# Attention visits of four and three tiles, one sigmoid split by banks, and PV with crossed heads, in a fused sigmoid-attention and SwiGLU kernel

## Chip, cores, metric

One core of one Trainium2 chip. The metric is device time in microseconds (us), the median of the runs of one kernel. Times of different kernels are compared through runs on the same chip in the same rounds.

## The reference, cut to what matters

```python
# q, k, v: (8 batches, 12 heads, 448, 64); w_gate, w_val: (768, 1536); w_out: (1536, 768)
scores = q @ k.T / sqrt(64) - log(448)
x      = sigmoid(scores) @ v                 # heads side by side: (3584, 768)
g      = x @ w_gate
out    = (g * sigmoid(g) * (x @ w_val)) @ w_out
```

Sigmoid attention has no row sums, so each tile of scores is independent: QK on TensorE, a sigmoid on ScalarE, PV on TensorE.

## The kernel before

Work comes in head groups `n` (four heads of one batch, 24 in all). A group has seven QK tiles of 64 keys each (per tile four 64x64 products side by side in the array), seven sigmoids, one PV. FFN units (`ffn1`: 12 matmuls into two banks, a gate on ScalarE and VectorE; `ffn2`: 24 matmuls) fill TensorE, and between them the program inserts *visits*: a few QK tiles, with PV of the group that was finished last.

All products write into a ring of four PSUM buffers of two banks each. A buffer can be written again once its readers are done.

```python
def attn_step(group, pvs):                     # one visit
    for part in (group[:2], group[2:]):
        scs = [(n, c, qk_tile(n, c)) for n, c in part]
        while pvs:
            pv(pvs.pop(0))
        for n, c, sc in scs:
            sig_tile(n, c, sc)                 # one ACTIVATE over both banks

def pv(n, two=False, at=None):
    ...
    out=P[h2 * 64:(h2 + 1) * 64, w, :S]        # head (h2, w): partitions by h2, bank by w
    ...
    for h2 in range(2):                        # x of a head pair wants partitions by w
        for w in range(2):
            x[w*64:(w+1)*64] <- P[h2*64:(h2+1)*64, w]      # four copies of 64x448
                # two (only the third PV): w == 1 on ScalarE, declared independent of w == 0

visits = [tiles[i:i + 3] for i in range(0, len(tiles), 3)]
...
    fn(*args)                                  # the FFN unit after a visit
    while post:
        trans_pe(post.pop())                   # Q, K of head groups 4 to 6 transposed on TensorE
```

Groups 0 to 2 run in a hand-ordered start, groups 3 to 5 beside the first batch's FFN; from group 7 on the transposes are done by DMA.

Of the kernel before, what the change touches and what calls it, by code (L numbers as in the profile page):

```python
# [10 lines left out]
FP16 = mybir.dt.float16  # L11
BF16 = mybir.dt.bfloat16
SIGM = mybir.ActivationFunctionType.Sigmoid
# [4 lines left out]
def kernel(  # L18
# [10 lines left out]
    nc = tc.nc  # L29
    ctx.enter_context(tc.manual_schedule())  # L30

    B, H, S, D = q.shape
    DM = H * D
    DFF = moe_w_gate.shape[1]
    C = S // D
    NJ = H // 4
    NP = H // 2
# [6 lines left out]
    qkscale = 1.0 / math.sqrt(D)  # L44
# [9 lines left out]
    xtp = ctx.enter_context(tc.tile_pool(name="xtp", bufs=12))  # L54
# [4 lines left out]
    sb_t = one.tile([128, 1], FP32, tag="sbias")  # L59
# [72 lines left out]
    def load(n, which, eng=None):  # L132
        st = stg.tile([128, 2, S], FP32, tag="stg", name=f"st{which}_{n}")
        (eng or nc.sync).dma_start(out=st, in_=src_of(n, which))  # L134
        qkv_st[(n, which)] = st

    def load_v(n):
        t = v16p.tile([128, 2, S], FP16, tag="v16", name=f"v16_{n}")
        nc.gpsimd.dma_start(out=t, in_=src_of(n, 2))  # L139
        v16[n] = t  # L140

    def cast(n, which, eng, lo=0, hi=C):
        st = qkv_st[(n, which)]
        if hi == C:
            qkv_st.pop((n, which))
        t = c16.tile([128, hi - lo, 2, D], BF16, tag="c16" if hi - lo == C else f"c16_{lo}", name=f"c16_{which}_{n}")
        q16[(n, which, lo)] = t
        eng.tensor_copy(  # L148
            out=t.rearrange("p c h d -> p h c d"),
            in_=st.rearrange("p h (c d) -> p h c d", c=C)[:, :, lo:hi, :],  # L150
        )

    def trans_dma(n, which):
        t = q16.pop((n, which, 0))
        d = qkT.tile([128, C, 128], BF16, tag=f"T{which}", name=f"T{which}_{n}")
        nc.sync.dma_start_transpose(out=d, in_=t.rearrange("p c h d -> p (c h d)"))
        for c in range(C):
            qT[(n, which, c)] = d[:, c]
        if which == 0:
            qT[(n, 0)] = d  # L160

    def trans_pe(n, parts=((0, 0, C), (1, 0, C))):

        D2 = Banked()
        ps = D2.t.bitcast(BF16).rearrange("p w (c i) -> p w c i", c=8)
        for i, (which, lo, hi) in enumerate(parts):
            t = q16.pop((n, which, lo))
            for c in range(hi - lo):
                D2.write(
                    nc.tensor.transpose(  # L170
                        out=ps[:, i, c, :], in_=t[:, c].rearrange("p h d -> p (h d)"), identity=idn
                    ),
                    i,
                )
        for i, (which, lo, hi) in enumerate(parts):
            tag = f"T{which}" if hi - lo == C else f"T{which}_{lo}"
            d = qkT.tile([128, hi - lo, 128], BF16, tag=tag, bufs=None if hi - lo == C else 1, name=f"T{which}_{n}_{lo}")
            D2.read(nc.vector.tensor_copy(out=d, in_=ps[:, i, :hi - lo, :]), i)  # L178
            for c in range(lo, hi):
                qT[(n, which, c)] = d[:, c - lo]  # L180
            if which == 0:
                qT[(n, 0)] = d
# [3 lines left out]
    xT = {}  # L186

    def qk_tile(n, c):
        sc = Banked().t
        qt, kt = qT[(n, 0)], qT[(n, 1, c)]  # L190
        for w in range(2):
            for h2 in range(2):
                r = slice(h2 * 64, h2 * 64 + 64)
                nc.tensor.matmul(  # L194
                    out=sc[w * 64:(w + 1) * 64, h2, :S],
                    lhsT=kt[r, w * 64:(w + 1) * 64],
                    rhs=qt[r, :, w * 64:(w + 1) * 64],
                    start=True,
                    stop=True,
                )  # L200
        return sc

    def sig_tile(n, c, sc):
        pt = ptp.tile([128, 2, S], FP16, tag="pt", name="pt")
        nc.scalar.activation(out=pt, in_=sc[:, :, :S], func=SIGM, bias=sb_t, scale=qkscale)  # L205
        pts[(n, c)] = pt

    def pv(n, two=False, at=None):
        b, j = divmod(n, NJ)
        P = Banked(at=at).t  # L210
        vt = v16.pop(n)
        for c in range(C):
            pt = pts.pop((n, c))
            for h2 in range(2):
                for w in range(2):
                    r = slice(w * 64, w * 64 + 64)
                    nc.tensor.matmul(  # L217
                        out=P[h2 * 64:(h2 + 1) * 64, w, :S],
                        lhsT=vt[r, h2, c * D:(c + 1) * D],
                        rhs=pt[r, h2, :],  # L220
                        start=(c == 0),
                        stop=(c == C - 1),
                    )
        for h2 in range(2):
            x = xtp.tile([128, S], FP16, tag="xT", name=f"xT_{b}_{2 * j + h2}")
            for w in range(2):
                o, i = x[w * 64:(w + 1) * 64, :], P[h2 * 64:(h2 + 1) * 64, w, :S]
                if two and w == 1:
                    cp = nc.scalar.copy(out=o, in_=i)
                    tc.declare_no_dep(cp.ins, group=f"half{n}_{h2}", reason="other partitions")  # L230
                else:
                    cp = nc.vector.tensor_copy(out=o, in_=i)  # L232
                    if two:
                        tc.add_to_no_dep_group(f"half{n}_{h2}", cp.ins)
            xT[(b, 2 * j + h2)] = x


    hT = {}
# [1 line left out]
    def ffn1_mm(D, b, f, prs):  # L240
        cs = slice((f % FW) * 128, (f % FW) * 128 + 128)
        for i, w16 in enumerate((wg16, wv16)):
            for pr in prs:
                D.write(
                    nc.tensor.matmul(  # L245
                        out=D.t[:, i, :S], lhsT=w16[f // FW][:, pr, cs], rhs=xT[(b, pr)],
                        start=(pr == 0), stop=(pr == NP - 1),
                    ),
                    i,
                )  # L250
# [92 lines left out]

    FIRST, PER = f1_end[0] - 5.0, 38.5
    tiles = [(n, c) for n in range(NJ, NQ) for c in range(C)]
    visits = [tiles[i:i + 3] for i in range(0, len(tiles), 3)]
    vtime = []
    for grp in visits:
        n, c = grp[0]
        b, j = divmod(n, NJ)  # L350
# [6 lines left out]
    def attn_step(group, pvs):  # L357
        for part in (group[:2], group[2:]):
            scs = [(n, c, qk_tile(n, c)) for n, c in part]
            while pvs:  # L360
                pv(pvs.pop(0))
            for n, c, sc in scs:
                sig_tile(n, c, sc)

    NPE = 2 * NJ + 1

# [1 line left out]
    V, G = nc.vector, nc.gpsimd  # L368
# [4 lines left out]
    for i in range(9):  # L373
        nc.tensor.matmul(out=ring[i % 4][:, i // 4 % 2, :], lhsT=warm[:, :128], rhs=warm, start=True, stop=True)
    cast(0, 0, V)
    cast(0, 1, V, 0, 2)
    trans_pe(0, ((0, 0, C), (1, 0, 2)))
    cast(0, 1, V, 2, C)

    def fetch(n):  # L380
        load(n, 0, G)
        load(n, 1, G)
        load_v(n)

    def ready(n):
        cast(n, 0, G)
        cast(n, 1, G)
        if n >= NPE:
            trans_dma(n, 0)
            trans_dma(n, 1)  # L390

    def chunk(n, c):
        sig_tile(n, c, qk_tile(n, c))
# [48 lines left out]

    k0 = ring_at[0] % 4
    early = [Banked("f")]
    for prs in (range(2), range(2, NP - 2)):
        ffn1_mm(early[0], 0, 0, prs)
    chunk(2, 5)
    chunk(2, 6)
    early.append(Banked("f"))
    ffn1_mm(early[1], 0, 1, range(NP - 2))  # L450
# [9 lines left out]

    post = []
    begin = {(n, c): [] for n in range(NJ, NQ) for c in (0, 4)}
    begin[(3, 0)] += [lambda: post.append(4)]
    begin[(3, 4)] += [lambda: ready(5)]
    begin[(4, 0)] += [lambda: post.append(5), lambda: fetch(6)]
    begin[(4, 4)] += [lambda: ready(6)]
    begin[(5, 0)] += [lambda: fetch(7)]
    begin[(5, 4)] += [lambda: post.append(6)]
    begin[(6, 0)] += [lambda: ready(7), lambda: fetch(8)]
# [15 lines left out]
    for dur, fn, args in units:  # L485
        if vi < len(visits) and tcur >= vtime[vi]:
            group = visits[vi]
            vi += 1
            pvs, pend = pend, []
            attn_step(group, pvs)  # L490
            for n, c in group:
                for act in begin.get((n, c), ()):
                    act()
                if c == C - 1:
                    pend.append(n)
        if pend and (
            fn is ffn1 and args[1] == 0 and (args[0], NP - 1) not in xT
            or vi == len(visits) and tcur >= vtime[-1] + 4.0
        ):
            for n in pend:  # L500
                pv(n)
            pend = []
        fn(*args)
        while post:
            trans_pe(post.pop())
        tcur += dur


# [28 lines left out]
```

## Time and profile before

| | |
|---|---|
| time, median (6 runs) | 434.64 us |
| span of the profiled run | 433.3 us |
| TensorE / VectorE / ScalarE busy | 418.9 / 220.6 / 209.9 us |
| sigmoids of scores | 168, mean 1006 ns |
| PV copies 64x448 on VectorE | 94, mean 622 ns |

The prediction below shows the lines of the profile and how they are read.

### The profile page before, as it was taken

What the parts mean: (1) busy time and instruction counts of PE and PEld (TensorE: products, weight loads), DVE (VectorE), ACT (ScalarE), POOL (GpSimd) and SP (SyncE); (2) the same over time, 40 slices, a digit from 0 to 9 for tenths busy, and PEclk for the clock granted to TensorE, in tenths of its full rate; (3) what the DMA queues carried; (4) which work ended last, traced back from release to release, by engine and by line L of the source; (5) the groups of instructions that cost most, each with busy time, mean ns of one, the idle gap of its engine ahead of it and who ended that gap; (6) DMA issues with size and microseconds to landing.
All of it is one profiled execution on the core that took longest, in us unless ns stands there. A gap on an engine that the chain in (4) does not pass through costs nothing.

```text
span 433.3 us, 7921 instructions
## 1 busy us (share of the span) xinstructions
PE 418.9 (97%) x3275; PEld 218.1 (50%) x3275; DVE 220.6 (51%) x366; ACT 209.9 (48%) x269; POOL 116.4 (27%) x166
## 2 busy tenths in 40 slices
PE   6889998999999999999999999999999999999995
PEld 2444444455555444444555544444555545555553
DVE  3736556465243557376343556476343367555322
ACT  3976784656345464646345465646435452222000
POOL 4554345230256454000156446000032100000000
PEclk9999999999999999999999999999999999999999
DMA  8999899999498998300198997500054200000234
GB/s 296 234 277 207 193 209 159 185 201 122 97 172 204 225 202 212 61 6 2 36 178 206 215 219 177 121 2 2 2 116 110 74 1 2 0 2 1 51 96 109
DMA packets 55940, 53.92 MB, mean 124 GB/s; under 512 B 33824, under 2 KB 50592, under 8 KB 55904
## 3 DMA queue, kind: packets, MB, share of 16 engines
q0 software_dynamic: 20896, 39.20, 41.5%
q1 hardware_dynamic: 34656, 13.67, 19.7%
q10 hardware_dynamic: 352, 0.56, 0.4%
q8 instruction: 25, 0.41, 0.4%
q14 instruction: 11, 0.09, 0.1%
HBM read 47.19 MB, written 11.01 MB: 134 GB/s over the span
## 4 chain that ended last, share of the span: by engine, by line
PE 91%; DVE 4%; ACT 3%; DMA 1%; issue 1%; DVEq 0%; ACTq 0%
PE ps_D L245 49%; PE ps_D L284 26%; PE ps_D L194 8%; PE ps_D L217 7%; ACT pt L205 2%; DVE xT L232 2%; DMA st<-in_q_dram 1%; PE ps_D L170 1%; DVE T L178 1%; DVE t L261 1%; DVE hT L265 1%; ACT s L259 0%; DVE c L148 0%; DVE oe L307 0%; ACT oe L303 0%
## 5 line engine op out<-in xcount | busy, mean ns | idle before, releaser
L205 ACT ACTIVATE pt<-ps_D,sb_t 128x896 f16<-128x896 f32 x168 | 157.0, 1006 | 94.4 <-PE ps_D L194 93.0
L245 PE MATMUL ps_D<-xT,wg 128*128 128x448 f16 x576 | 126.1, 353 | 2.6 <-DVE xT L232 1.8
L245 PE MATMUL ps_D<-xT,wv 128*128 128x448 f16 x576 | 125.3, 352 | 0.0
L284 PE MATMUL ps_D<-wo,hT 128*128 128x384 f16 x672 | 112.1, 326 | 0.3 <-DVE hT L265 0.3
L261 DVE TENSOR_TENSOR t<-ps_D,s 128x448 f16<-128x448 f32 x96 | 59.7, 622 | 86.1 <-ACT s L259 85.6
L259 ACT ACTIVATE s<-ps_D 128x448 f16<-128x448 f32 x96 | 52.3, 545 | 94.3 <-PE ps_D L245 92.5
L284 PEld LDWEIGHTS <-hT 128*128 128x128 f16 x672 | 64.6, 98 | 47.2 <-issue 5.6
L245 PEld LDWEIGHTS <-wv 128*128 128x128 f16 x576 | 56.3, 98 | 54.5 <-issue 2.0
L245 PEld LDWEIGHTS <-wg 128*128 128x128 f16 x576 | 53.5, 98 | 59.6 <-issue 14.0
L232 DVE CAST xT<-ps_D 64x448 f16<-64x448 f32 x94 | 58.5, 622 | 29.0 <-PE ps_D L217 28.0
L314 DVE TENSOR_SCALAR osb<-ps_D 128x384 f32<-128x384 f32 x55 | 30.6, 557 | 72.9 <-PE ps_D L284 72.7
L265 DVE SCALAR_TENSOR_TENSOR hT<-ps_D,t 128x448 f16<-128x448 f32 x96 | 60.0, 625 | 10.4 <-DVE t L261 0.5
L324 POOL DMA_DIRECT2D out_dram<-osb x42 | 22.3, 536 | 150.9 <-DVE osb L314 150.9
L148 POOL CAST c<-st 128x896 bf16<-128x896 f32 x41 | 37.8, 935 | 66.9 <-issue 31.1
L194 PE MATMUL ps_D<-T,T 64*64 64x448 bf16 x672 | 48.7, 367 | 3.2 <-DVE T L178 1.3
L217 PE MATMUL ps_D<-pt,v 64*64 64x448 f16 x672 | 36.0, 350 | 1.2 <-DVE hT L265 0.7
L194 PEld LDWEIGHTS <-T 64*64 64x64 bf16 x672 | 15.9, 107 | 27.5 <-issue 20.4
L217 PEld LDWEIGHTS <-v 64*64 64x64 f16 x672 | 19.9, 107 | 13.6 <-issue 2.5
L139 POOL DMA_DIRECT2D v<-in_v_dram x24 | 17.7, 737 | 0.1
L134 POOL DMA_DIRECT2D st<-in_k_dram x20 | 14.7, 735 | 3.3 <-DVE T L178 3.3
L134 POOL DMA_DIRECT2D st<-in_q_dram x20 | 14.6, 732 | 0.6 <-DMA v<-in_v_dram 0.6
L303 ACT ACTIVATE oe<-ps_D 64x384 f32<-64x384 f32 x1 | 0.5, 484 | 27.9 <-PE ps_D L284 27.9
(21 smaller groups left out, 48.2 us busy)
## 6 DMA issues: line engine op xcount, KB each, us to landing
st<-in_q_dram POOLq DMA_DIRECT2D x20, 448.0 KB, 5.1
st<-in_k_dram POOLq DMA_DIRECT2D x20, 448.0 KB, 7.6
out_dram<-osb POOLq DMA_DIRECT2D x42, 192.0 KB, 3.1
v<-in_v_dram POOLq DMA_DIRECT2D x24, 224.0 KB, 8.9
wg<-in_moe_w_gate_dram POOLq DMA_DIRECT2D x4, 576.0 KB, 14.6
wv<-in_moe_w_val_dram POOLq DMA_DIRECT2D x4, 576.0 KB, 15.0
wo<-in_moe_w_out_dram POOLq DMA_DIRECT2D x4, 576.0 KB, 15.3
out_dram<-osb SPq DMA_DIRECT2D x12, 192.0 KB, 2.7
```

Source lines behind the costliest of these rows:

```text
L134: (eng or nc.sync).dma_start(out=st, in_=src_of(n, which))
L148: eng.tensor_copy(out=t.rearrange("p c h d -> p h c d"), in_=st.rearrange("p h (c d) -> p h c d", c=C)[:, :, lo:hi, :],)
L194: nc.tensor.matmul(out=sc[w * 64:(w + 1) * 64, h2, :S], lhsT=kt[r, w * 64:(w + 1) * 64], rhs=qt[r, :, w * 64:(w + 1) * 64], start=True, st ...
L205: nc.scalar.activation(out=pt, in_=sc[:, :, :S], func=SIGM, bias=sb_t, scale=qkscale)
L217: nc.tensor.matmul(out=P[h2 * 64:(h2 + 1) * 64, w, :S], lhsT=vt[r, h2, c * D:(c + 1) * D], rhs=pt[r, h2, :], start=(c == 0), stop=(c == C ...
L232: cp = nc.vector.tensor_copy(out=o, in_=i)
L245: nc.tensor.matmul(out=D.t[:, i, :S], lhsT=w16[f // FW][:, pr, cs], rhs=xT[(b, pr)], start=(pr == 0), stop=(pr == NP - 1),),
L259: D.read(nc.scalar.activation(out=s16, in_=D.t[:, 0, :S], func=SIGM), 0)
L261: D.read(nc.vector.tensor_tensor(out=t1, in0=D.t[:, 0, :S], in1=s16, op=MULT), 0)
L265: nc.vector.scalar_tensor_tensor(out=hT[(b // 2, f)][:, b % 2, :], in0=D.t[:, 1, :S], scalar=HSC, in1=t1, op0=MULT, op1=MULT),
L284: nc.tensor.matmul(out=D.t[:, half, :hw], lhsT=h[:, m * 128:(m + 1) * 128], rhs=wo16[f // FW][:, f % FW, half * hw:(half + 1) * hw], start ...
L314: nc.vector.tensor_scalar(out=osb[:, hs], in0=D.t[:, half, :hw], scalar1=HREC, scalar2=None, op0=MULT),
```

## The change

Its intent: fewer trips of TensorE from FFN into attention (42 visits instead of 49), no new wait behind the larger visits, three PV copies instead of four, and less waiting in the start.

"Crossed heads" means: `x` wants the two heads of a pair one above the other. PV now writes each pair into one bank, so the first pair can be moved by one copy of all 128 partitions. The second pair lies there in the opposite order and still takes two half copies; by this crossing the four products of a key tile keep four different combinations of input half and output half.

The core of the diff, with cuts marked `...` and the copies and orders in short form:

```diff
@@ qk_tile, sig_tile
-        nc.scalar.activation(out=pt, in_=sc[:, :, :S], func=SIGM, ...)
+        if split:                       # second tile of a visit of four
+            for h2 in range(2):
+                sd.read(nc.scalar.activation(out=pt[:, h2, :], in_=sc[:, h2, :S], ...), h2)
+        else:
+            nc.scalar.activation(out=pt, in_=sc[:, :, :S], func=SIGM, ...)
@@ pv
-                        out=P[h2 * 64:(h2 + 1) * 64, w, :S],
+                        out=P[g:g + 64, h2, :S],          # g = (w ^ h2) * 64
-        four copies of 64x448, with two: w == 1 on ScalarE, declared independent
+        nc.vector.tensor_copy(out=x, in_=P[:, 0, :S])      # head pair 0 whole
+        for w in range(2):                                 # head pair 1, halves crossed
+            (nc.scalar.copy if two else nc.vector.tensor_copy)(
+                out=x[w*64:(w+1)*64], in_=P[(1-w)*64:(2-w)*64, 1, :S])
@@ visits
-    visits = [tiles[i:i + 3] for i in range(0, len(tiles), 3)]
+    visits = [tiles[i:i + d] for i in range(0, len(tiles), C) for i, d in ((i, 4), (i + 4, 3))]
@@ start
-    cast(0, 1, V, 0, 2)
-    trans_pe(0, ((0, 0, C), (1, 0, 2)))
-    cast(0, 1, V, 2, C)
+    cast(0, 1, nc.scalar, 0, 2)
+    cast(0, 1, nc.scalar, 2, C)
+    trans_pe(0, ((0, 0, C), (1, 0, 2)), (V, nc.scalar))
@@ before the third PV
-    for prs in (range(2), range(2, NP - 2)):
-        ffn1_mm(early[0], 0, 0, prs)
+    ffn1_mm(early[0], 0, 0, range(2))
     chunk(2, 5)
+    ffn1_mm(early[0], 0, 0, range(2, NP - 2))
@@ transposes of groups 4 to 6: behind the visit, not behind the FFN unit after it
+            while post:
+                trans_pe(post.pop())
         ...
         fn(*args)
-        while post:
-            trans_pe(post.pop())
```

More of the change, by code (lines that the diff above doesn't have):

```diff
@@ L147, in cast @@
         q16[(n, which, lo)] = t
-        eng.tensor_copy(
+        (eng.copy if eng is nc.scalar else eng.tensor_copy)(
             out=t.rearrange("p c h d -> p h c d"),
@@ L160, in trans_dma, with trans_pe @@
             qT[(n, 0)] = d
-    def trans_pe(n, parts=((0, 0, C), (1, 0, C))):
+    def trans_pe(n, parts=((0, 0, C), (1, 0, C)), engs=(nc.vector, nc.vector)):
         D2 = Banked()
@@ L177, in trans_pe @@
             d = qkT.tile([128, hi - lo, 128], BF16, tag=tag, bufs=None if hi - lo == C else 1, name=f"T{which}_{n}_{lo}")
-            D2.read(nc.vector.tensor_copy(out=d, in_=ps[:, i, :hi - lo, :]), i)
+            copy = engs[i].copy if engs[i] is nc.scalar else engs[i].tensor_copy
+            D2.read(copy(out=d, in_=ps[:, i, :hi - lo, :]), i)
             for c in range(lo, hi):
@@ L188, in qk_tile @@
     def qk_tile(n, c):
-        sc = Banked().t
+        sd = Banked()
+        sc = sd.t
         qt, kt = qT[(n, 0)], qT[(n, 1, c)]
@@ L200, in qk_tile, with sig_tile @@
                 )
-        return sc
-    def sig_tile(n, c, sc):
+        return sd
+    def sig_tile(n, c, sd, split=False):
+        sc = sd.t
         pt = ptp.tile([128, 2, S], FP16, tag="pt", name="pt")
-        nc.scalar.activation(out=pt, in_=sc[:, :, :S], func=SIGM, bias=sb_t, scale=qkscale)
+        if split:
+            for h2 in range(2):
+                sd.read(
+                    nc.scalar.activation(out=pt[:, h2, :], in_=sc[:, h2, :S], func=SIGM, bias=sb_t, scale=qkscale), h2
+                )
+        else:
+            nc.scalar.activation(out=pt, in_=sc[:, :, :S], func=SIGM, bias=sb_t, scale=qkscale)
         pts[(n, c)] = pt
@@ L216, in pv @@
                     r = slice(w * 64, w * 64 + 64)
+                    g = (w ^ h2) * 64
                     nc.tensor.matmul(
-                        out=P[h2 * 64:(h2 + 1) * 64, w, :S],
+                        out=P[g:g + 64, h2, :S],
                         lhsT=vt[r, h2, c * D:(c + 1) * D],
@@ L223, in pv @@
                     )
-        for h2 in range(2):
-            x = xtp.tile([128, S], FP16, tag="xT", name=f"xT_{b}_{2 * j + h2}")
-            for w in range(2):
-                o, i = x[w * 64:(w + 1) * 64, :], P[h2 * 64:(h2 + 1) * 64, w, :S]
-                if two and w == 1:
-                    cp = nc.scalar.copy(out=o, in_=i)
-                    tc.declare_no_dep(cp.ins, group=f"half{n}_{h2}", reason="other partitions")
-                else:
-                    cp = nc.vector.tensor_copy(out=o, in_=i)
-                    if two:
-                        tc.add_to_no_dep_group(f"half{n}_{h2}", cp.ins)
-            xT[(b, 2 * j + h2)] = x
+        x = xtp.tile([128, S], FP16, tag="xT", name=f"xT_{b}_{2 * j}")
+        nc.vector.tensor_copy(out=x, in_=P[:, 0, :S])
+        xT[(b, 2 * j)] = x
+        x = xtp.tile([128, S], FP16, tag="xT", name=f"xT_{b}_{2 * j + 1}")
+        for w in range(2):
+            o, i = x[w * 64:(w + 1) * 64, :], P[(1 - w) * 64:(2 - w) * 64, 1, :S]
+            if two:
+                nc.scalar.copy(out=o, in_=i)
+            else:
+                nc.vector.tensor_copy(out=o, in_=i)
+        xT[(b, 2 * j + 1)] = x
     hT = {}
@@ L361, in attn_step @@
                 pv(pvs.pop(0))
-            for n, c, sc in scs:
-                sig_tile(n, c, sc)
+            for i, (n, c, sc) in enumerate(scs):
+                sig_tile(n, c, sc, split=len(group) == 4 and part[0] == group[0] and i == 1)
     NPE = 2 * NJ + 1
@@ L462 @@
     begin = {(n, c): [] for n in range(NJ, NQ) for c in (0, 4)}
-    begin[(3, 0)] += [lambda: post.append(4)]
-    begin[(3, 4)] += [lambda: ready(5)]
-    begin[(4, 0)] += [lambda: post.append(5), lambda: fetch(6)]
-    begin[(4, 4)] += [lambda: ready(6)]
+    begin[(3, 4)] += [lambda: post.append(4), lambda: ready(5)]
+    begin[(4, 0)] += [lambda: fetch(6)]
+    begin[(4, 4)] += [lambda: post.append(5), lambda: ready(6)]
     begin[(5, 0)] += [lambda: fetch(7)]
```

## The prediction

> **What bounds the kernel now.** I read the page first: busy shares, chain of waits, groups.
>
> ```profile
> PE 418.9 (97%) x3275; PEld 218.1 (50%) x3275; DVE 220.6 (51%) x366; ACT 209.9 (48%) x269; POOL 116.4 (27%) x166
> ...
> PE 91%; DVE 4%; ACT 3%; DMA 1%; issue 1%; DVEq 0%; ACTq 0%
> ```
>
> TensorE is busy in 97% of 433.3 us and is 91% of the chain. VectorE and ScalarE stand at half, so work taken off them pays only where TensorE waits for them. Where is that? The table by stretches says (columns: length, then busy time of PE, PEld, DVE, ACT, POOL with counts, clock, DMA share, GB/s):
>
> ```profile
> 6.00:16.00 10.00, 7.87 (x80) 4.26 (x84) 6.08 (x12) 7.13 (x8) 8.27 (x10) 1.00 1.15 312
> 16.00:27.00 11.00, 8.26 (x124) 5.17 (x116) 7.56 (x13) 10.37 (x12) 5.52 (x7) 1.00 1.24 246
> ...
> 37.00:73.00 36.00, 33.26 (x327) 17.30 (x327) 22.06 (x37) 26.46 (x32) 14.05 (x19) 1.00 1.10 195
> 73.00:205.00 132.00, 132.00 (x1039) 67.26 (x1038) 70.06 (x115) 71.37 (x92) 41.21 (x57) 1.00 0.77 141
> ...
> 210.00:358.00 148.00, 148.00 (x1202) 77.18 (x1200) 73.23 (x122) 73.82 (x92) 40.34 (x60) 1.00 0.50 107
> ```
>
> Three regimes. To 27 us ScalarE is nearly full (10.37 of 11 us): the first sigmoids set the pace. From 37 to 73 us TensorE waits 2.7 us in small pieces. From 73 us on it never waits (except 0.25 us at 207): only fewer or cheaper TensorE work counts. The clock is 1.00 throughout.
>
> The chain in order of time (start, length, what) shows what one attention visit costs in the full stretch:
>
> ```profile
> 139.33 0.19 PE ps_D L194 x4
> 139.52 6.92 PE ps_D L245 x36
> 146.44 0.69 PE ps_D L194 x12
> 147.13 4.65 PE ps_D L245 x24
> 151.77 0.50 PE ps_D L194 x8
> 152.28 1.32 PE ps_D L217 x28
> 153.60 0.19 PE ps_D L194 x4
> ...
> 358.24 43.24 PE ps_D L245 x228
> 401.48 27.31 PE ps_D L284 x168
> ```
>
> L194 is QK (four 64x64 products side by side in 0.19 us), L217 is PV, L245 and L284 are the two FFN matmuls. Undisturbed, one L245 matmul takes 43.24/228 = 0.190 us. After a visit, 36 of them take 6.92 instead of 6.83, and 24 take 4.65 instead of 4.55: 0.10 lost. Three QK tiles after FFN work take 0.69 instead of 3 x 0.19 = 0.57: 0.12 lost. Behind PV a QK takes 0.19 with no loss. So each trip from FFN into attention and back costs about 0.22 us, whatever it carries.
>
> The ramp's largest single wait, again the chain:
>
> ```profile
> 68.62 1.35 PE ps_D L217 x28
> 69.99 0.62 DVE xT L232
> 70.62 0.62 DVE xT L232
> 71.27 0.63 DVE xT L232
> 71.91 0.64 DVE xT L232
> 72.59 3.75 PE ps_D L245 x19
> ```
>
> FFN of the second batch needs the last heads, whose four half-tile copies stand in a row; TensorE loses about 1.6 us here (it could have passed this point at 71.0).
>
> **What the Trainium skill says.** "TensorEngine Tiling (Array Packing)", Key Properties: changing the tiling mode drains TensorE. The 0.22 us per trip agrees. The same page, Gotcha 1: different row tiles cannot use one PSUM bank at the same time; the new PV does put both row tiles into one bank, at different partitions. "PSUM — Partial Sum Buffer", section on bank collisions, narrows it: between row tiles it is bank x 32-partition quadrant that collides, and different quadrants of one bank are independent. The new layout keeps to that; no run yet shows which page holds here. "ScalarE: Activation LUTs", Table sets: copy is in every table set, so moving casts to ScalarE costs no reload. The trace agrees: it has ScalarE copies and one table load of 1.28 us in all.
>
> **The change part by part.** I compared the built order of TensorE instructions of both kernels.
>
> *Visits of 4 and 3.* 147 QK tiles in 42 visits instead of 49; counts of matmuls are equal (3275). Seven trips fewer x 0.22 = 1.5 us. One falls in the ramp (7 visits instead of 8 before the second batch starts, carrying 25 tiles instead of 24), six in the full stretch: 1.3 us sure gain, if no wait appears. I check that on a visit of four with PV, time 0 at its start: QK 0.12 to 0.5, PV to 1.8, QK to 2.2, FFN from 2.3. ScalarE's sigmoids (1.0 us each, from the group's mean 1006 ns) run from 0.5: the first ends at 1.5, before the fourth QK needs its buffer at 2.0. The second would end at 2.5, after FFN wants the buffer at 2.3; split by banks its first half ends near 2.1 and FFN's first six matmuls (1.1 us) use that bank. So the split removes a wait of 0.25 that visits of four would add. It costs 2 x 545 - 1006, about 0.1 us, on an engine half idle. All four sigmoids end at 4.6, the next gate follows, its FFN buffer is wanted again three units later. No wait.
>
> *Crossed heads.* Four copies of 64x448 (622 ns) become one of 128x448 and two of 64x448. A 128x448 operation on VectorE also takes 622 ns (the gate's product), so a PV's copies take 1.9 instead of 2.5 us. That is 24 x 0.62 = 15 us of VectorE time, of which only waits count: at the second batch's start 0.63; before that, in the ScalarE stretch, 0.26 at 20.0 us (a QK waits for PV's buffer, ScalarE for the QK).
>
> *Casts on ScalarE.* The first K cast and its transpose copy (283 and 280 ns) leave VectorE. The cast was hidden behind the transposes; the copy was last (7.00 to 7.82 for two): the first QK comes 0.27 us sooner, and ScalarE, which bounds this stretch, starts sooner by it.
>
> *QK (2,5) earlier.* ScalarE stood idle for 1.06 us at 26.6 because these tiles' QK stood behind FFN pieces. Walking the new order with the durations above, the third PV starts near 28.4 instead of 29.34. So with casts and copies the first full FFN unit starts about 0.95 us sooner (34.58 before). Its weights were issued at 14.1 and 17.0 and landed 15.1 and 15.5 us later (the view of transfers), at 32.5 at the latest, so no transfer stops it.
>
> *Ramp from there to the second batch.* Same walk, in the old kernel's clock. Against: the first visit has four tiles and the fourth needs the buffer of an FFN unit whose gate ends at 38.6 (VectorE works off four gates in a row): about 1.0 us lost, where the old kernel lost 0.3. The second and third PE transposes now stand right behind a visit and need the buffer of the FFN unit before it, whose gate waits behind four sigmoids: 0.9 us each. For: the old waits of 0.75 at 42, 0.7 at 50 and 0.2 at 59 go, and the 1.6 at 72 falls to 0.7. Sum of waits 3.5 new against 3.55 old; with the trip saved (0.22) that is about 0.3 gain, and the extra tile already done is 0.2 for later.
>
> Sum: 0.95 + 0.3 + 0.2 + 1.3 = 2.75 us. 434.4 - 2.8 = 431.6 us.
>
> **The rivals.** (a) Row tiles in one bank: if TensorE serialised them, a PV of 28 would take up to 2.6 instead of 1.32 us: 24 x 1.3 = +31 us, 465 us. For it speaks the tiling page's wording, and that both kernels' QK and the old PV keep one bank per row tile; against it the PSUM page. I give it 3%. (b) The ramp gives all back: four-tile visits pile sigmoids before the gates and transposes behind them, as reckoned 1.8 us for two transposes and 1.0 for the first visit; if each is half a microsecond worse and the startup gain stays in the DMA (share 1.1 to 1.24 there), 433.5. (c) The sigmoid burst also delays FFN buffers in the full stretch: a wait of 0.3 at each of 20 visits with PV would be +6 us, 437. Against: the walk leaves 0.2 us at the tightest place (split half against FFN start), and ScalarE is 54% busy there. (d) The early gains are larger, the transposes meet free buffers: 430.
>
> **Range and chances.** The sure term is 1.3; the others come from a walk with errors of some 0.3 at each of five places. Predicted 431.6 us, 8 in 10 between 430.0 and 433.2. A gain over 2% (8.7 us) would need more than all of TensorE's waits after 27 us removed: 1%. Within 2%: 95%. Slower by over 2%, through (a) or a strong (c): 4%.
>
> **What would show it.** In the full stretch: still no TensorE wait, PV of 28 in 1.32 us (else (a)), visits of four with PV of about 2.2 us. In the ramp: third PV near 28.4; first full FFN unit near 33.6; waits before the fourth QK of the first visit and before the second and third transposes; second batch's FFN resuming near 71.3 with a wait near 0.7 for the copies. A TensorE wait for ScalarE's sigmoid before L245 in the full stretch would prove me wrong, as would a gain after 73 us far from 1.3 to 1.5.

## The result, and the profile after

431.29 us, median of 6 runs (430.99 to 432.09), against 434.64 us. The ratio is 0.9927, 95% interval 0.9914 to 0.9939. Ratios are the mean time of one kernel's fast runs over that of the other's of the same rounds, so not quite the ratio of the medians quoted. The output is correct. The predicted 431.6 us and the range held; the parts of the sum did not all hold.

The runs of either kernel fall in two groups: 434.24 to 434.36 and 434.92 to 435.10 before, 430.99 to 431.32 and 432.00 to 432.09 after (last section). The medians mix them three to three before and four to two after; by the medians of like groups the gain is 3.1 us in the lower and 3.0 in the upper.

The page of the changed kernel, the rows of busy time and of the chain by engine:

```profile
PE 416.3 (97%) x3275; PEld 218.4 (51%) x3275; DVE 205.5 (48%) x339; ACT 212.7 (50%) x293; POOL 116.5 (27%) x166
...
PE 90%; DVE 4%; ACT 4%; DMA 1%; issue 1%; DVEq 0%; ACTq 0%
```

VectorE lost the 15 us that were reckoned (24 x 0.62), ScalarE gained 3. That these count only where TensorE waited is seen in the table by stretches (columns as in the prediction):

```profile
6.00:16.00 10.00, 7.35 (x93) 4.14 (x95) 5.44 (x9) 8.58 (x11) 8.23 (x10) 0.83 1.16 311
16.00:27.00 11.00, 9.09 (x122) 5.29 (x113) 6.04 (x10) 10.94 (x13) 6.06 (x8) 1.00 1.24 246
...
37.00:71.00 34.00, 32.31 (x319) 16.80 (x319) 19.59 (x32) 27.19 (x38) 11.24 (x15) 1.00 1.06 198
...
210.00:358.00 148.00, 148.00 (x1203) 77.73 (x1202) 70.09 (x116) 75.10 (x103) 39.77 (x59) 1.00 0.51 107
```

TensorE is still full from 71 us on. From 16 to 27 us ScalarE is now busy for 10.94 of 11 us, where it was 10.37. The ramp (in this view from 37 us until the second batch's FFN runs), whose end has moved from 73 to 71 us, holds 1.7 us of TensorE idle instead of 2.7.

A visit of four with PV in the chain of the changed kernel (start, length, what):

```profile
84.03 0.50 PE ps_D L196 x8
84.53 1.32 PE ps_D L227 x28
85.85 0.38 PE ps_D L196 x8
86.23 6.92 PE ps_D L255 x36
```

It takes 2.20 us, as reckoned, and FFN goes on at once. The 28 matmuls of PV take 1.32 us as before, with both row tiles in one bank: rival (a) is out.

The wait at the second batch's start, same view:

```profile
68.43 0.62 DVE xT L236
69.08 0.62 DVE xT L244
69.72 0.63 DVE xT L244
70.39 6.03 PE ps_D L255 x31
```

Three copies instead of four, and TensorE resumes at 70.39 instead of 72.59 us; half of these 2.20 us, 1.10, were gained before the ramp (first full FFN unit at 33.48 instead of 34.58), part of them by the chance of the start.

One of the new waits, that of the second transposes behind their visit, same view:

```profile
50.53 0.58 ACT s L269
51.13 0.64 DVE t L271
51.86 0.64 DVE hT L275
52.54 0.55 PE ps_D L170 x7
```

The gate of the FFN unit before the visit runs late (behind the sigmoids), and the seven K transposes wait for the bank that VectorE reads last. In the list of waits this and its twin stand with 0.2 us each, and the fourth QK of the first visit with 0.9 us for VectorE.

**Where the time went, by stretches.** For every kernel I read five lengths between starts of TensorE's work in its timeline. They repeat within 0.02 us between profiled runs wherever the program of the stretch is the same (one exception, below under more warm-up), while the time up to the first PV varies by 1.3 us between runs of the very same instructions (last section), so it is left out.

| stretch (us) | before | changed | difference |
|---|---|---|---|
| B: first PV to second PV | 6.86 | 6.47 | -0.39 |
| C: second PV to third PV | 6.95 | 6.65 | -0.30 |
| D: third PV to the first full FFN unit | 5.24 | 5.49 | +0.25 |
| E: ramp, from there to w_val of the second batch's first unit | 38.20 | 37.10 | -1.10 |
| F: full stretch, from there to ScalarE's last eviction | 356.03 | 354.40 | -1.63 |
| sum | 413.28 | 410.11 | -3.17 |

The runs give the same within their spread: 431.29 - 434.64 = -3.35, 0.73% of 434.6 is 3.2, and like groups give 3.1 and 3.0. The experiments take the parts apart in this table.

### The profile page after: what moved, and what is told of

Its sections match the earlier page's. It is cut to its first block, busy times and chain, and to the rows that moved or that the text cites. A ratio compares the mean times of both kernels' runs of the same rounds, so it can differ in the third digit from the quotient of the medians.

```text
span 429.4 us, 7929 instructions
## 1 busy us (share of the span) xinstructions
PE 416.3 (97%) x3275; PEld 218.4 (51%) x3275; DVE 205.5 (48%) x339; ACT 212.7 (50%) x293; POOL 116.5 (27%) x166
## 4 chain that ended last, share of the span: by engine, by line
PE 90%; DVE 4%; ACT 4%; DMA 1%; issue 1%; DVEq 0%; ACTq 0%
PE ps_D L255 48%; PE ps_D L294 26%; PE ps_D L196 7%; PE ps_D L227 7%; ACT pt L214 2%; PE ps_D L170 1%; DVE hT L275 1%; DMA st<-in_q_dram 1%; DVE t L271 1%; DVE xT L236 1%; DVE xT L244 1%; ACT s L269 1%; ACT pt L211 1%; DVE T L179 0%; ACT xT L242 0%
## 5 line engine op out<-in xcount | busy, mean ns | idle before, releaser
L214 ACT ACTIVATE pt<-ps_D,sb_t 128x896 f16<-128x896 f32 x147 | 139.5, 1015 | 85.7 <-PE ps_D L196 85.5
L255 PE MATMUL ps_D<-xT,wg 128*128 128x448 f16 x576 | 125.9, 353 | 1.2 <-DVE xT L244 0.6
L255 PE MATMUL ps_D<-xT,wv 128*128 128x448 f16 x576 | 125.3, 352 | 0.0
L255 PEld LDWEIGHTS <-wv 128*128 128x128 f16 x576 | 56.3, 98 | 53.6 <-issue 1.2
L255 PEld LDWEIGHTS <-wg 128*128 128x128 f16 x576 | 53.7, 98 | 57.5 <-issue 11.3
L196 PE MATMUL ps_D<-T,T 64*64 64x448 bf16 x672 | 47.0, 361 | 3.6 <-ACT T L179 1.1
L236 DVE CAST xT<-ps_D 128x448 f16<-128x448 f32 x24 | 15.0, 624 | 30.1 <-PE ps_D L227 23.3
L244 DVE CAST xT<-ps_D 64x448 f16<-64x448 f32 x46 | 28.6, 622 | 0.7
L211 ACT ACTIVATE pt<-ps_D,sb_t 128x448 f16<-128x448 f32 x42 | 24.2, 631 | 0.0
```

Source lines behind the costliest of these rows:

```text
L196: nc.tensor.matmul(out=sc[w * 64:(w + 1) * 64, h2, :S], lhsT=kt[r, w * 64:(w + 1) * 64], rhs=qt[r, :, w * 64:(w + 1) * 64], start=True, st ...
L211: nc.scalar.activation(out=pt[:, h2, :], in_=sc[:, h2, :S], func=SIGM, bias=sb_t, scale=qkscale), h2
L214: nc.scalar.activation(out=pt, in_=sc[:, :, :S], func=SIGM, bias=sb_t, scale=qkscale)
L244: nc.vector.tensor_copy(out=o, in_=i)
L255: nc.tensor.matmul(out=D.t[:, i, :S], lhsT=w16[f // FW][:, pr, cs], rhs=xT[(b, pr)], start=(pr == 0), stop=(pr == NP - 1),),
```

## The experiments

My theory before them: the trips explain F; crossed heads, casts and the earlier QK explain B to E. The rival: one part carries all, and others cost. Eight kernels undo a part, isolate one or take an order away; three more build a better version from what they showed, and the changed kernel ran once more as a control.

**Visits of three again** (49 visits, hence no split; all else as changed).

```diff
-    visits = [tiles[i:i + d] for i in range(0, len(tiles), C) for i, d in ((i, 4), (i + 4, 3))]
+    visits = [tiles[i:i + 3] for i in range(0, len(tiles), 3)]
```

> The changed kernel with visits of three again (49 instead of 42, so no split either), all else as changed. Theory (a trip between FFN and attention costs 0.22 us whatever it carries, and no wait hangs on it): the stretch without waits grows by 6 trips, 1.3 us; in the ramp one trip more (0.2) but the wait of 0.87 before the fourth QK of the first visit goes. Sum +0.8 to +1.5 over the changed kernel, about 432.2 to 432.8, ratio to before near 0.996. Rival (the gain lies in the ramp alone, visits don't matter): same as the changed kernel within 0.3.

432.59 us, ratio 0.9957 (0.9944 to 0.9969). F is 356.03, the value of the kernel before; E is 36.84, 0.26 shorter than in the changed kernel. So visits of four and three with the split gain 1.63 in the full stretch and cost 0.26 in the ramp. Six trips of 0.22 and the tile done earlier (0.2) are 1.5 of the 1.63; 0.1 is not accounted for.

**No split.**

```diff
-    sig_tile(n, c, sc, split=len(group) == 4 and part[0] == group[0] and i == 1)
+    sig_tile(n, c, sc)
```

> The changed kernel with the second sigmoid of a visit of four in one piece. Theory: in a visit with PV the FFN unit behind it wants the second QK tile's buffer at 2.2 us of the visit, the sigmoid in one piece would leave it some 0.15 to 0.25 later, so each of 20 visits with PV waits that long: +3 to +5 us, 434.5 to 436, slower than or level with before; PE waits for the sigmoid at the end of such visits in the full stretch. Rival (ScalarE's sigmoids overlap enough, the split is not needed): within 0.5 us of the changed kernel.

434.39 us, ratio 0.9998 (0.9985 to 1.001): the whole gain is gone. F is 357.60, 3.20 longer. Of the 20 visits of four with PV, 17 lie in the full stretch (the other three in the ramp), so that is 0.19 for each; from first QK to FFN such a visit takes 2.39 to 2.46 us here and 2.20 in the changed kernel. The chain of this kernel at the end of such a visit:

```profile
98.55 0.34 PE ps_D L196 x4
...
98.92 0.59 ACT pt L214
...
99.83 1.01 ACT pt L214
...
100.88 2.43 PE ps_D L255 x12
```

FFN (L255) now follows a sigmoid (L214); in the changed kernel the FFN unit at 86.23 followed QK. But E is 36.79, 0.31 shorter: in the ramp the split costs a little. There each visit of four with PV takes 0.19 longer without it too, but each of the two transposes right behind a visit, with its visit, takes 0.34 less (in TensorE's timeline, from the visit's first QK to the FFN unit behind: 1.64 instead of 1.98).

**Visits of four and three alone, in the kernel before** (old copies, no split).

```diff
-    visits = [tiles[i:i + 3] for i in range(0, len(tiles), 3)]
+    visits = [tiles[i:i + d] for i in range(0, len(tiles), C) for i, d in ((i, 4), (i + 4, 3))]
```

> The old kernel with the visits of four and three alone: old PV copies, no split. Theory: 7 trips saved, -1.5, against a wait of 0.15 to 0.25 in each of 20 visits with PV for want of the split (+3 to +5), and the four copies of PV (2.5 us) meet the third FFN buffer: slower than before by 1.5 to 3.5 us, about 436 to 438. Rival (trips alone decide): faster than before by 1.5.

435.42 us, ratio 1.0021 (1.0007 to 1.0034): slower, though by 1.0 instead of the 1.5 to 3.5 expected. F is 357.62, the same as without split above. E is 37.70, 0.50 shorter than before, so beside the old place of the transposes and without the split larger visits gain in the ramp. In the full stretch they pay only together with the split.

**Old PV layout and copies.**

```diff
-    out=P[g:g + 64, h2, :S]; one copy of 128x448 and two of 64x448
+    out=P[h2 * 64:(h2 + 1) * 64, w, :S]; four copies of 64x448, as before
```

> The changed kernel with the old PV layout and its four half copies. Theory: only waits on the copies count: 0.6 at the second batch's start, about 0.3 near 20 us, while the third PV's copies, split over both engines without an order, gain 0.4: +0.3 to +0.9 us over the changed kernel if the copies' 0.6 us per PV is hidden elsewhere. In the full stretch the old copies end 4.5 us into the visit and the second FFN unit behind it wants that buffer at 4.5: if it waits 0.1 in each of 20 visits, +2 more. Rival (VectorE's 15 us count): +5 or more.

434.04 us, ratio 0.9986 (0.9973 to 0.9998). Against the changed kernel: B 6.86 (+0.39), C 7.26 (+0.61), D 5.24 (-0.25), E 38.14 (+1.04), F 354.93 (+0.53); sum +2.32. This was the largest surprise: I had expected +0.3 to +0.9 for the start and ramp and perhaps up to 2 in the full stretch. It is not the 15 us of VectorE either, of which some five sixths stay hidden. The list of waits of this kernel names two of its places:

```profile
PE ps_D L196 <- DVE xT L241: 1.3, 2, 0.7
...
PE ps_D L170 <- DVE hT L274: 0.8, 2, 0.6
```

QK waits twice in the start, 1.3 us in all, for PV's copies (at 20 and 26.7 us), which the changed kernel's list does not have: that is B and C. Of the 1.04 in E the lists name 0.7: the transposes behind a visit wait 0.8 for VectorE's gates, against 0.4, and FFN waits 0.9 for the last heads, against 0.6. By the starts in the timelines the two places hold all of it: at the first of the two transposes the second half starts 1.15 us after the first (53.42, 54.57), against 0.73 (51.81, 52.54), so 0.42; and at the second batch FFN resumes 2.34 us after its first matmuls (70.71, 73.05), against 1.70 (68.69, 70.39), so 0.64. The list counts less of the last, as part of that wait lies before an earlier matmul. The 0.53 of the full stretch is in no list; in the chain from 80 us on, three FFN units behind a visit take 6.96 us in 7 of 11 places where the changed kernel's take 6.92 in all 11. That is 0.28; the rest is not located.

**First K casts and the transpose copy on VectorE again.**

```diff
-    cast(0, 1, nc.scalar, 0, 2)
-    cast(0, 1, nc.scalar, 2, C)
-    trans_pe(0, ((0, 0, C), (1, 0, 2)), (V, nc.scalar))
+    cast(0, 1, V, 0, 2)
+    trans_pe(0, ((0, 0, C), (1, 0, 2)))
+    cast(0, 1, V, 2, C)
```

> The changed kernel with the first K casts and the transpose copy on VectorE again. Theory: the first QK comes 0.27 us later, ScalarE bounds the stretch behind it, and all later work moves by it: +0.2 to +0.4 us, third PV near 28.3 instead of 28.0. Rival: hidden behind later waits, 0.

431.18 us, ratio 0.9925 (0.9911 to 0.9938): the part brought nothing. From the first transpose to the first QK it is 1.48 us here (5.77 to 7.25) and 1.74 us in the run of the first experiment (5.86 to 7.60), which has the new casts and as fast first transposes. So with the new casts the first QK comes 0.26 us later. The line that tells why is ScalarE's timeline, first of the changed kernel:

```profile
7.32 0.37 ACT L179 COPY T<-ps_D 128x256 bf16<-128x256 bf16 x1 [0.81 <-DVE T L179]
```

ScalarE's copy waited for VectorE's copy (L179), although both only read, from two banks. The program orders them because both belong to one buffer, and 0.37 us behind the other copy is later than VectorE's own 0.28.

**QK (2,5) behind the first FFN piece again.**

```diff
-    ffn1_mm(early[0], 0, 0, range(2))
-    chunk(2, 5)
-    ffn1_mm(early[0], 0, 0, range(2, NP - 2))
+    for prs in (range(2), range(2, NP - 2)):
+        ffn1_mm(early[0], 0, 0, prs)
+    chunk(2, 5)
```

> The changed kernel with QK of tile (2,5) behind all of the first FFN piece again. Theory: ScalarE idles about 0.5 to 1.0 us near 25.7 and the third PV comes 0.4 to 0.9 later, near 28.5 to 28.9; everything behind moves by it: +0.4 to +0.9 us. Rival: the wait of VectorE's gates swallows it, 0.

430.67 us, ratio 0.9911 (0.9898 to 0.9925): the old order is the better one. C is 6.32, 0.33 shorter; nothing else moves. ScalarE does idle, 0.43 us, but the third PV does not wait for it. TensorE's timeline, first of the changed kernel, then of this one:

```profile
24.88 0.38 PE L196 MATMUL ps_D<-T,T 64*64 64x448 bf16 x4
25.20 0.55 PE L255 MATMUL ps_D<-xT,wg 128*128 128x448 f16 x2
...
26.06 0.38 PE L196 MATMUL ps_D<-T,T 64*64 64x448 bf16 x4
...
27.99 1.52 PE L227 MATMUL ps_D<-pt,v 64*64 64x448 f16 x28
```

```profile
25.56 0.57 PE L196 MATMUL ps_D<-T,T 64*64 64x448 bf16 x8
...
27.68 1.52 PE L227 MATMUL ps_D<-pt,v 64*64 64x448 f16 x28
```

Two QK tiles apart are two trips into attention, at 0.22 each; together they are one. In addition the first of them waits for a buffer that PV's copies leave at 24.84. TensorE sets this stretch, not ScalarE. With the old copies it was the same: C is 6.95 before and 7.26 with old copies and new order, +0.31.

**Transposes one FFN unit behind the visit again.**

```diff
-            while post:                       # right behind the visit
-                trans_pe(post.pop())
         ...
         fn(*args)
+        while post:
+            trans_pe(post.pop())
@@ and groups 4 and 5 are put on the list a visit sooner
-    begin[(3, 4)] += [post 4, ...];  begin[(4, 4)] += [post 5, ...]
+    begin[(3, 0)] += [post 4];       begin[(4, 0)] += [post 5, ...]
```

> The changed kernel with the transposes of heads 4 to 6 one FFN unit behind the visit again, as before the change. Theory: the changed place waits about 0.35 to 0.5 at two transposes; the old place waits too (in the old kernel 0.75 and 0.7), so +0.3 to +1.0 us over the changed kernel, all of it between 36 and 68 us. Rival: the place is indifferent, within 0.3; or the new place is worse (two transposes wait for the gate behind four sigmoids, as I feared): -0.5.

431.06 us, ratio 0.9923 (0.991 to 0.9935). E is 36.99, 0.11 shorter. My expectation of +0.3 to +1.0 was a miss; the place is nearly indifferent, each place has its wait.

**The third PV's half copies on ScalarE not ordered behind VectorE's whole copy** (they read the other bank).

```diff
-        nc.vector.tensor_copy(out=x, in_=P[:, 0, :S])
+        cp = nc.vector.tensor_copy(out=x, in_=P[:, 0, :S])
+        if two:
+            tc.add_to_no_dep_group(f"half{n}", cp.ins)
...
-                nc.scalar.copy(out=o, in_=i)
+                cp = nc.scalar.copy(out=o, in_=i)
+                tc.declare_no_dep(cp.ins, group=f"half{n}", reason="the other bank")
```

> The changed kernel, but the third PV's two half copies on ScalarE no longer wait for the whole copy on VectorE (they read the other bank). In the changed kernel ScalarE's first half copy began at 30.29, when VectorE's copy had ended, instead of 29.63 as PV ended; the last FFN pieces waited 0.4 for it. Theory: first gate and first full FFN unit 0.4 to 0.45 earlier, and as VectorE's row of four gates sets the fourth QK of the first visit, that moves too: -0.4 us, 430.8. Rival: swallowed, 0.

430.90 us, ratio 0.9923 (0.9908 to 0.9937). By time alone this is unclear against 431.29. D is 5.24 instead of 5.49, and the lines of ScalarE's timeline, of the changed kernel and of this one, show the order go:

```profile
30.29 1.06 ACT L242 CAST xT<-ps_D 64x448 f16<-64x448 f32 x2 [2.73 <-DVE xT L236]
```

```profile
30.52 1.06 ACT L244 CAST xT<-ps_D 64x448 f16<-64x448 f32 x2 [2.00 <-PE ps_D L227]
```

The release is now PV itself. It brings 0.25, not the 0.4 expected. (The start lies later only because this run's third PV began at 28.95 instead of 27.99, by chance of the clock.)

**What pays, put together.** The diffs of four experiments at once (casts on VectorE, old order of QK (2,5), transposes late, half copies free), and the split only from group 6 on:

```diff
-    split=len(group) == 4 and ...
+    split=n >= 2 * NJ and len(group) == 4 and ...
```

> The changed kernel with what did not pay undone and one order taken away: first K casts on VectorE, QK of tile (2,5) behind the first FFN piece, transposes one FFN unit behind the visit, split only from head group 6 on, and the third PV's half copies on ScalarE no longer ordered behind the whole copy. From the stretches of the single runs: second to third PV 0.3 shorter, third PV to first full FFN unit 0.25 shorter, ramp 0.1 + 0.3 shorter, full stretch as changed (354.4). Theory (the stretches add): 0.9 to 1.1 us under the changed kernel, about 430.2. Rival (they hang on one another, the gates on VectorE swallow most): 0.5 or less.

430.55 us, ratio 0.991 (0.9897 to 0.9924); the control of the same rounds has 431.12, so 0.57 less. The stretches are B 6.47, C 6.32, D 5.24, E 37.07, F 354.39: sum 409.49 against 410.11, 0.62 less. C and D add as expected, but E does not: the 0.11 and 0.31 of the single edits do not add up in the ramp (0.03 in all). The theory of adding held for two terms of four.

**Casts on ScalarE, with its transpose copy freed as well**, else as the version before.

```diff
+            if engs[1] is nc.scalar:        # in trans_pe: bank 0 by VectorE, bank 1 by ScalarE
+                if i == 0: tc.add_to_no_dep_group(f"tcopy{n}", cp.ins)
+                else:      tc.declare_no_dep(cp.ins, group=f"tcopy{n}", reason="the other bank")
```

> As the version before, but the first K casts and transpose copy on ScalarE, and that copy not ordered behind VectorE's (in the changed kernel it began at 7.32, when VectorE's copy had ended, though it reads the other bank). Theory: this is why the casts on ScalarE brought nothing; freed, the first QK comes 0.25 to 0.4 sooner and the time falls by 0.1 to 0.3 against that version. Rival: ScalarE's copy is slower (0.37 against 0.28) and casts arrive later: no gain.

429.95 us, ratio 0.9902 (0.9888 to 0.9915), the lowest median of all. The first QK comes 1.28 us after the first transpose (5.89 to 7.17), against 1.47 with casts on VectorE (6.15 to 7.62) and 1.74 in the changed order. ScalarE's copy now begins at 6.60, while VectorE's runs:

```profile
6.60 0.37 ACT L179 COPY T<-ps_D 128x256 bf16<-128x256 bf16 x1
```

So the idea of the casts was sound and the order undid it. That this version is faster than the one before by time is not settled (the intervals overlap); that it is faster than the changed kernel is likely (0.9902 against 0.9927 of the control, 1.2 us between medians). In the profiled runs of these two versions the stretches from the first PV on have the same sum (409.49), so the gain lies in the start, where chance is mixed in: from 9.3 to 12.6 us the granted clock is 0.50 in the version before and 1.00 in this one.

**More warm-up.** The first of these versions (casts on VectorE) with a tenth warm-up matmul and four small ones between the first transposes and the first QK.

```diff
-    for i in range(9):
+    for i in range(10):
         nc.tensor.matmul(out=ring[i % 4][...], lhsT=warm[:, :128], rhs=warm, ...)
     ...
     trans_pe(0, ((0, 0, C), (1, 0, 2)))
+    for i in range(4):
+        nc.tensor.matmul(out=ring[3][:, i % 2, :128], lhsT=warm[:, :128], rhs=warm[:, :128], ...)
```

> As the version before the last, with a tenth warm-up matmul and four small ones between the first transposes and the first QK. Observation: runs of one kernel fall in two groups 0.7 to 0.8 us apart; in the slow ones the first transposes take 1.14 instead of 0.68 us for nine and the mean clock reads 1.000, because no faster clock is granted before about 13 us. Theory[...]: with TensorE kept busy through 5 to 8 us nearly every run starts fast, the slow group vanishes, the median falls 0.1 to 0.3. Rival: the phase stays chance, two groups as before, and the extra matmuls add 0.1 to 0.3.

430.19 us, ratio 0.9901 (0.9886 to 0.9917), 0.36 under the version without. But all four runs of that version happened to fall in the fast group, so whether the slow group vanishes was not tested; and in this kernel's profiled run the first PV took 2.41 us instead of 1.52 and B was 7.06 instead of 6.47: from 14.2 to 18.1 us the granted clock was 0.57. It stays open.

**Control**, the changed kernel again.

> The changed kernel itself once more beside these three, for a comparison on the same chip in the same call: 431.0 to 431.4 in the fast group, 432.0 in the slow one, ratio 0.9925.

431.12 us, ratio 0.9927 (0.9915 to 0.994): as expected; one run of five at 431.98.

## Why the prediction was right, and where it was not

**Trips and visits of four: right.** 1.3 of trips and 0.2 for the extra tile, 1.5 for the full stretch; measured 1.63 (with the split), and visits of three gave exactly those 1.63 back. A visit of four with PV takes 2.20 us, no wait follows.

**Split: right in mechanism, a little too large in size.** I reckoned 0.25 per visit, though my own times (2.5 and 2.3 us) give 0.2; measured 0.19 (3.20 over the 17 visits in the full stretch; I had counted all 20, here and in rival (c)). Without the split the second sigmoid ends 2.35 us after the visit's start and FFN begins at 2.40, where it begins at 2.20 with the split: both times came earlier than reckoned, so they nearly cancel. I put sigmoids 1.0 us apart, the mean duration. In the changed kernel three in a row take 2.80: one of 1.01 and two steps of 0.90. The Trainium skill, "ScalarE: Activation LUTs", section What ACT_TABLE_LOAD costs, says that neighbouring activations overlap by some 93 ns; the trace agrees with 0.11. The step, not the duration, is what a queue adds.

**Crossed heads: mis-sized.** The term was 0.63 at the second batch plus 0.26 at 20 us, 0.89. Undoing the part costs 2.32 over the stretches. I had counted waits that the old profile names. The one at the second batch was right: 0.64. The 0.62 of each PV also lay inside waits named after others: 0.39 before the second PV (0.26 reckoned) and 0.61 before the third, where the copies hold a buffer that QK wants; 0.42 at a transpose in the ramp; and 0.53 in the full stretch. Only D goes the other way (0.25), by the order put on the third PV's copies, which I did not see in the diff although the old lines that declared independence are removed in it.

**Casts: wrong.** "The first QK comes 0.27 us sooner": it comes 0.26 later for like clock, as the two copies are ordered. Reading which semaphore each of the two copies waits for in the built order would have shown it.

**QK (2,5) earlier: wrong sign.** I saw ScalarE idle for 1.06 us and took it for the cause of the third PV's time. TensorE's own work set it; the new order adds a trip and costs 0.33.

**Ramp: waits too large.** I predicted 3.5 us of waits after against 3.55 before and a gain of 0.3. E fell by 1.10. The fourth QK waited 0.87 (1.0 reckoned), and the copies cost 0.75 in the way I counted them (0.7): FFN could have passed at 69.64 and did at 70.39. The two transposes lose some 0.5 us each, not 0.9: without waits the second FFN unit behind would start at about 52.45 (visit's end near 51.65, 0.8 for 14 transposes) and it starts at 52.93. Sigmoids 0.9 apart bring the gates forward, as above; that this is the reason is not shown. That crossed heads give 1.04 there is shown by the fourth experiment. Visits of four with the split cost 0.26 by the first (E 36.84 without them); by the second it is the split that costs them, as without it E is 36.79.

**The absolute times: luck.** The prediction named the first full FFN unit near 33.6, and it came at 33.48. But up to the first PV the start varies by 1.3 us, and this run's first PV came 0.66 sooner than the old kernel's (14.87, 15.53), which no run ties to the change. From there to the first full FFN unit the gain is 0.44 (B, C and D), where 0.95 less 0.27 of the casts were reckoned. Nor was the clock "1.00 throughout": at 6 us the old kernel's first transposes ran slow (last section).

So the total was right partly by errors that cancel. Crossed heads were 1.43 too small (2.32 against 0.89). The QK order was 0.75 too favourable: its share of the 0.95 for the start was 0.95 - 0.27 - 0.26 = 0.42, and it costs 0.33. The casts' 0.27 did not come at all. Measured one by one the parts nearly add up: crossed heads 2.32, visits with the split 1.63 - 0.26, QK order -0.33, place of the transposes -0.11, in all 3.25 against 3.17. The rivals: (a) did not occur, (b) and (c) did not, though without the split something like (c) does happen (434.39), and (d), free buffers for the transposes, comes nearest to the ramp, although each transpose still loses 0.5.

## What to carry to other kernels

When TensorE is full, count its changes of tiling mode: each trip (0.22 us here) cost the same whatever it carried, so make visits as large as the buffers allow, and find which reader frees the first buffer that is wanted next. Splitting that one reader by banks may be worth more than the trips. Moving one of two reads of a buffer to another engine pays only if the program does not order the two; look at what each waits for. And an idle engine next to a late event is no proof that it causes it: undo that part alone.

## What the Trainium skill lacked or had wrong

- "TensorEngine Tiling (Array Packing)", Gotcha 1, is too strict as worded: PV with both row tiles in one bank, in different partition halves, runs correctly and takes 1.32 us for 28 matmuls, as before. "PSUM — Partial Sum Buffer", section "PSUM bank collisions raise a hardware error", quotes the same strict wording, and beside it states as measured that two row tiles collide on one bank and quadrant. It does not say that row tiles in different quadrants of one bank are free; the runs show it for halves of 64 partitions.
- The same tiling page, Key Properties, names the drain at a change of mode without a size. Here a change cost 0.12 us on the way into 64x64 tiles and 0.10 back, and six trips fewer gave, with the tile done earlier, 1.63 us in the full stretch.
- "TensorE: Matmul & The Clock Gate", Part 1, says that the activity window runs free, so the start is chance. The runs agree: the first PV of one and the same start began at 14.52, 14.87 and 15.82 us, and runs of one kernel fall in two groups (431.0 to 431.3 and 432.0 to 432.1 us for the changed one); that the two groups are the two kinds of start fits the profiled runs and is not proven. The page warns that the clock's trace events can be unreliable, but not that the granted clock in the profile can hide a slow start. From 6 to 16 us the kernel before reads 1.00 and the changed one 0.83, yet it is the former whose matmuls are slow: nine first transposes take 1.14 us there and 0.81 here (TensorE's timelines, kernel before, then changed):

```profile
6.03 1.14 PE L170 MATMUL ps_D<-idn,c 128*128 128x128 bf16 x9 [0.82 <-DVE c L148]
```

```profile
5.86 0.81 PE L170 MATMUL ps_D<-idn,c 128*128 128x128 bf16 x9 [0.65 <-DVE c L148]
```

  In the trace of the kernel before, the first grant on record lies 14 us after the start; the mean of the clock seems to leave out what has no record. Durations are the safer witness, and stretches after the start the safer comparison.
